# Short second halves of two experts: three products in two 64-column tiles instead of rounded part and rest side by side

## The chip, the cores and the metric

The kernel runs on one core of a Trainium2 chip. The metric is the device time of one execution in microseconds, lower is better. TensorE multiplies a stationary operand (its weights, loaded by a LDWEIGHTS) with a moving one and writes to PSUM; VectorE and ScalarE work between PSUM and SBUF; GpSimd (POOL in the rows) issues the indirect DMAs; SyncE (SP) issues the others.

## What is computed

Two stages, cut to what matters here. First a decaying linear attention over 2 batches, 8 heads, 768 positions and 64 dimensions; its output is 1536 tokens of 512 values. Then a mixture of 8 experts: each token goes to one expert `e` (its own best one or the one of the token before it), and

```python
h = np.maximum(x[b, s] @ w1[e], 0.0)     # 512 -> 1024
out[b, s] = p[e] * (h @ w2[e])           # 1024 -> 512, p the softmax of the logits
```

All inputs and outputs are f32.

## The kernel before

The matmuls of the experts run in f16. Each f32 operand is split into a rounded part (`hi`, `hh`) and the rest that rounding left (`lo`, `hl`), and a product of two operands is the sum of three f16 products: rounded by rounded, rounded by rest, rest by rounded.

The tokens are sorted into lists of up to 256 places an expert, gathered by an indirect DMA and turned by a DMA transpose. The first two experts are taken as they come, the other six are ranked by the number of their tokens; `CAPS` gives the places that each position in this order computes: 256 for the first three, then 244, 228, 214, and 192 for the last two, positions 6 and 7. A list is worked on in two halves, places 0 to 127 and the others. At positions 6 and 7 the second half has 192 - 128 = 64 places; `stacked(e)` is true for these two alone.

For each position, in the order of the program:

- `up(e, f)`, for 8 blocks `f` of 128 hidden values: twelve matmuls (L764) into one PSUM tile of 128 hidden values by the list's places. ScalarE writes `hh`, the positive part in f16, and VectorE writes the rest `hl`. Where `stacked(e)`, ScalarE's instruction stands at L774, and VectorE's is two (L777): the rest of places 0 to 127 goes to `hl`, and that of places 128 to 191 into the 64 free columns of `hh` right behind the rounded part of the same places. So 128 columns of `hh` hold rounded part and rest of the short second half side by side.
- `down(e, hf, f)`, for the half `hf` and the same 8 blocks: an ordinary half has three matmuls a block (L823), with 128 (or fewer) columns of `hh` or `hl` as weights and 512 columns of `w2` moving. The short second half of a stacked position has two (L814, L815): the 128 columns side by side, against the rounded `w2` and against its rest. Partitions 0 to 63 of the PSUM tile then hold the sum from the rounded part, and 64 to 127 that from the rest.
- `store(e, hf)`: scales by the probability and scatters the rows by an indirect DMA. For the short half ScalarE first copies partitions 64 to 127 (L844), VectorE adds the two halves (L845) and scales (L846).

At positions 6 and 7 the short second half comes ahead of the first half. At position 7, the last, the first half is computed in two parts of 256 columns, so that storing the first part overlaps the second. The order of everything is the order of the program text: a schedule by hand (`ORDER`) up to the first experts, and the loops at the end of the program from there. Weights are loaded by SyncE, rounded by ScalarE (L161) and their rest is taken by VectorE (L169), a few pieces behind each block.

In the attention part, earlier in the program, f32 matmuls use less than the whole array: L469 (scores by values) and L516 (the state) have 64 columns of weights each and write in turn to partitions 0 to 63 and 64 to 127 of one PSUM bank. L428 is a full-width f32 matmul (a transpose) of 128 moving columns.

Of the kernel before, what the change touches and what calls it, by code (L numbers as in the profile page):

```python
# [11 lines left out]
AF = mybir.ActivationFunctionType  # L12
ALU = mybir.AluOpType
# [4 lines left out]
P = 128  # L18
HP = P // 2
# [9 lines left out]
KF = F // P  # L29
# [77 lines left out]
def moe_kernel(ctx: ExitStack, tc, q, k, v, w_gate, w_local, w1, w2, cst, out):  # L107
    nc = tc.nc
# [73 lines left out]
    def ready(u, i):  # L182
        while any(tuple(t[:2]) == (u, i) for t in todo):
            split_some(1)
# [127 lines left out]
    with ExitStack() as both:  # L312
# [74 lines left out]
        def bank(b):  # L387
            pool, tag = BANKS[b]
            return pool.tile([P, NP, P], F32, tag=tag, name="tr")
# [273 lines left out]
        def rows(e, hf):  # L663
            return CAPS[e] - P if hf else P
# [56 lines left out]
        XX, HH, PO, RELU = {}, {}, {}, ([], [])  # L721
# [3 lines left out]
        def half(what, e, hf):  # L725

            t_ = what[e, hf] if (e, hf) in what else what[e]
            return t_ if (e, hf) in what else t_[..., hf * P : (hf + 1) * P]
# [14 lines left out]
        def up(e, f, hf=None, part=None):  # L743

            pair_, n_ = (f % 2, P) if hf is not None else (0, CAPS[e])
            first, last = part != 1, part != 0
            if f == 0 and first:
                if e < FEW and hf == 0:
                    HH[e, 0] = [
                        ap_.tile([P, KF, P], F16, tag="eh", name=f"{n}{e}_0", bufs=4) for n in ("hh", "hl")  # L750
                    ]
                else:
                    HH[e] = [mp[0].tile([P, KF, CAP], F16, tag=n, name=f"{n}{e}", bufs=2) for n in ("hh", "hl")]
            if first and pair_ == 0:
                third = hf is None and f % 3 == 2
                HH["ps"] = (ps_1 if third else ps_sc).tile([P, 2 * P], F32, tag="lgb" if third else "sc", name="h")
            ready(2 * e, 7)
            xx = XX[e] if hf is None else half(XX, e, hf)
            wh, wl = units[2 * e]
            ps, fs = HH["ps"], slice(f * P, (f + 1) * P)  # L760
            terms = [(kk, a, b_) for kk in range(KD) for a, b_ in ((wh, 0), (wh, 1), (wl, 0))]
            for n in range(0 if first else 6, 12 if last else 6):
                kk, a, b_ = terms[n]
                nc.tensor.matmul(  # L764
                    ps[:, pair_ * P : pair_ * P + n_], lhsT=a[:, kk, fs], rhs=xx[:, b_, kk, :n_],
                    start=(n == 0 and pair_ == 0), stop=(n == 11), skip_group_check=True,
                )
            if not last or (hf is not None and pair_ == 0):
                return
            if hf is None:  # L770
                hh, hl = (h_[:, f, :n_] for h_ in HH[e])
                ps = ps[:, :n_]
                if stacked(e):
                    nc.scalar.activation(hh, ps, AF.Relu)  # L774
                    both_ = ((hl[:, :P], slice(0, P)), (HH[e][0][:, f, P + HP :], slice(P, n_)))
                    for to, cols in both_:
                        nc.vector.scalar_tensor_tensor(to, ps[:, cols], 0.0, hh[:, cols], ALU.max, ALU.subtract)  # L777
                    return
            else:
                ps = ps.rearrange("p (a b) -> p a b", a=2)  # L780
                hh, hl = (h_[:, f - 1 : f + 1, :] for h_ in halves(e, hf))
            relu = [
                lambda: nc.scalar.activation(hh, ps, AF.Relu),  # L783
                lambda: nc.vector.scalar_tensor_tensor(hl, ps, 0.0, hh, ALU.max, ALU.subtract),  # L784
            ]
            if e < FEW and hf == 0:
                for to, op in zip(RELU, relu):
                    to.append(op)
                return
            for op in relu:  # L790
                op()

        def halves(e, hf):
            return HH[e, hf] if (e, hf) in HH else [h_[..., hf * P : (hf + 1) * P] for h_ in HH[e]]

        def stacked(e):

            return e >= FEW and CAPS[e] - P == HP

        def down(e, hf, f, part=None):  # L800
            ready(2 * e + 1, f)
            wh, wl = units[2 * e + 1]
            hh, hl = halves(e, hf)
            if f == 0:
                if part is not None:
                    to = bank("ys"[part]).rearrange("p a b -> p (a b)")[:, : DM // 2]
                    PO[e, hf] = PO.get((e, hf), []) + [to]
                elif hf == 0 and mp:
                    PO[e, hf] = ps_1.tile([P, DM], F32, tag="y", name="o")
                else:  # L810
                    PO[e, hf] = ps_tr.tile([P, DM], F32, tag="tr", name="o")
            if hf and stacked(e):
                po, a = PO[e, hf], HH[e][0][:, f, P:]
                nc.tensor.matmul(po, lhsT=a, rhs=wh[:, f, :], start=(f == 0), stop=(f == KF - 1), skip_group_check=True)  # L814
                nc.tensor.matmul(po, lhsT=a, rhs=wl[:, f, :], start=False, stop=(f == KF - 1), skip_group_check=True)  # L815
                return
            m = rows(e, hf)
            po = (PO[e, hf] if part is None else PO[e, hf][part])[:m]
            cols = slice(0, DM)
            if part is not None:  # L820
                cols = slice(part * DM // 2, (part + 1) * DM // 2)
            for n, (a, b_) in enumerate(((hh, wh), (hh, wl), (hl, wh))):
                nc.tensor.matmul(  # L823
                    po, lhsT=a[:, f, :m], rhs=b_[:, f, cols], start=(f == 0 and n == 0), stop=(f == KF - 1 and n == 2)
                )
# [37 lines left out]
        for e in range(FEW):  # L863
            fillers += [lambda e=e, f=f, h=h: up(e, f, 0, h) for f in range(KF) for h in range(2)]
            fillers += [lambda e=e, f=f: down(e, 0, f) for f in range(KF)]
# [45 lines left out]
        for e in range(FEW):  # L911
            if e + 1 < FEW:
                transposed(e + 1, 1)
            transposed(e + 2, 0)
            transposed(e + 2, 1)
            for f in range(KF):
                up(e, f, 1)
                split_some(1, 2 * e + 3)
                if e == 0 and f == 3:
                    fill_table(ptab, T["prhs"], 0, NC, 2 * E)  # L920
                    LST["pt"] = ranked(cp, probs(cp, ptab, 2.0 ** -(SH + SW + SP), ""), "ptr")
                    for n in range(FEW):
                        store(n, 0)
            queue(2 * e + 5)
            for f in range(KF):
                down(e, 1, f)
                split_some(1, 2 * e + 4)
            store(e, 1)
            queue(2 * e + 6)
        for e in range(FEW, LAST):  # L930
            if e + 2 < E:
                transposed(e + 2, 0)
                transposed(e + 2, 1)
            for f in range(KF):
                up(e, f)
                split_some(1, 2 * e + 3)
            queue(2 * e + 5)
            for n, hf in enumerate((1, 0) if stacked(e) else (0, 1)):
                if e + 1 == E and n == 1:
                    for part in range(2):  # L940
                        for f in range(KF):
                            down(e, hf, f, part)
                    store(e, hf)
                    break
                for f in range(KF):
                    down(e, hf, f)
                    if f % 2 == 1:
                        split_some(1, 2 * e + 4)
                store(e, hf)
            queue(2 * e + 6)  # L950
# [5 lines left out]
    with tc.If(nmore > 0), tc.For_i(0, nmore, 1), ExitStack() as lo_:  # L956
# [12 lines left out]
        for e in range(E):  # L969
# [18 lines left out]
            for f in range(KF):  # L988
                ps = pa.tile([P, CAP], F32, tag="h2p", name="h2p")
                for kk in range(KD):  # L990
                    nc.tensor.matmul(
                        ps, lhsT=wa[:, kk, f * P : (f + 1) * P], rhs=x2[:, kk, :],
                        start=(kk == 0), stop=(kk == KD - 1),
                    )
                nc.scalar.activation(h2[:, f, :], ps, AF.Relu)
            for hf in range(2):
                po = pa.tile([P, DM], F32, tag="tr2", name="o2")
                for f in range(KF):
                    nc.tensor.matmul(
                        po, lhsT=h2[:, f, hf * P : (hf + 1) * P], rhs=wb[:, f, :],  # L1000
                        start=(f == 0), stop=(f == KF - 1),
# [33 lines left out]
```

## Time and profile before

| | us |
|---|---|
| time, median of 3 runs | 268.12 (262.58 to 271.2) |
| the profiled execution's own time | 261.32 |
| its span, first to last instruction | 259.5 |
| TensorE matmul busy | 234.5 (90%) |
| weight loads busy | 176.3 (68%) |
| VectorE busy | 161.0 (62%) |
| ScalarE busy | 131.1 (51%) |
| GpSimd busy | 64.3 (25%) |

The rows come from one execution, and start at its first instruction. A matmul's own length in a row is longer than the step from one start to the next, since matmuls are pipelined and their ends are modelled; what a stream of them costs is read from starts. Weight loads (PEld) run beside matmuls. In a row of a timeline, neighbours of one line are merged: the start of the first, the time from it to the last end, and their count behind an x. A form such as 128*64 128x512 is the rows by columns of the weights, then the partitions and columns that move.

### The profile page before, as it was taken

The numbers are of one execution on the slowest core, as the hardware profiler recorded it, in microseconds if no ns is written. First come the engines' busy times: TensorE is split into PE (matmuls) and PEld (weight loads), VectorE is DVE, ScalarE is ACT, GpSimd is POOL, SyncE is SP. The second block draws the span as 40 slices with busy tenths as digits, with TensorE's granted clock in tenths as the row PEclk, the third lists the DMA queues.
The fourth block names the chain that finished last, engine by engine and source line by source line (L and its number), as shares of the span: only waits on it lengthen the run. The fifth ranks groups of instructions, "written<-read, shape, count | busy, mean of one in ns | idle before, by whom it ended". The sixth has DMA issues, their size and how long they took to land. (4 is left out here: it accounts for less than half of the span.)

```text
span 259.5 us, 6195 instructions
## 1 busy us (share of the span) xinstructions
PE 234.5 (90%) x2420; PEld 176.3 (68%) x2420; DVE 161.0 (62%) x383; ACT 131.1 (51%) x262; POOL 64.3 (25%) x69
## 2 busy tenths in 40 slices
PE   8588888867998989899999999999999999999970
PEld 2477667756887865858667847947947947849650
DVE  1247669877789878205997963965864865922210
ACT  2139877556442121213896763765765765803210
POOL 2440541624360104314025212042101103011020
PEclk9779999996899999999999999999999999999996
DMA  6999999999899744999999999999999994101001
GB/s 166 199 324 360 335 289 276 267 346 226 212 211 199 193 135 154 338 119 174 362 379 269 381 260 254 397 292 340 404 160 399 270 301 151 25 12 40 4 12 45
DMA packets 74004, 60.20 MB, mean 232 GB/s; under 512 B 51820, under 2 KB 58220, under 8 KB 73968
## 3 DMA queue, kind: packets, MB, share of 16 engines
q1 hardware_dynamic: 70992, 52.39, 74.9%
q0 software_dynamic: 2976, 7.35, 9.4%
q8 instruction: 21, 0.34, 0.6%
q14 instruction: 15, 0.12, 0.1%
HBM read 47.66 MB, written 6.91 MB: 210 GB/s over the span
## 5 line engine op out<-in xcount | busy, mean ns | idle before, releaser
L169 DVE SCALAR_TENSOR_TENSOR lo<-stg,hi 128x512 f16<-128x512 f32 x128 | 85.4, 701 | 16.0 <-ACT hi L161 13.2
L161 ACT ACTIVATE hi<-stg 128x512 f16<-128x512 f32 x128 | 73.7, 621 | 9.9 <-DMA stg<-in_moe_w_dram 9.9
L764 PE MATMUL h<-xx,hi 128*128 128x128 f16 (+5 forms) x640 | 77.8, 242 | 0.0
L764 PE MATMUL h<-xx,lo 128*128 128x128 f16 (+5 forms) x320 | 71.7, 242 | 0.0
L764 PEld LDWEIGHTS <-hi 128*128 128x128 f16 x640 | 55.9, 98 | 3.8 <-issue 0.3
L853 POOL DMA_INDIRECT out_dram<-ob,sidx x16 | 18.4, 1148 | 93.4 <-ACT ob L852 26.4
L823 PE MATMUL o<-hi,hl 128*128 128x512 f16 (+3 forms) x104 | 39.4, 379 | 1.1 <-DVE hl L784 1.1
L823 PEld LDWEIGHTS <-hh 128*128 128x128 f16 (+3 forms) x240 | 24.6, 103 | 21.9
L823 PE MATMUL o<-hi,hh 128*128 128x512 f16 (+3 forms) x104 | 39.4, 379 | 0.0
L823 PE MATMUL o<-lo,hh 128*128 128x512 f16 (+3 forms) x104 | 39.4, 379 | 0.0
L784 DVE SCALAR_TENSOR_TENSOR hl<-h,hh 128x256 f16<-128x256 f32 (+3 forms) x48 | 19.5, 407 | 22.9 <-ACT hh L783 22.5
L764 PEld LDWEIGHTS <-lo 128*128 128x128 f16 x320 | 31.3, 98 | 0.6
L783 ACT ACTIVATE hh<-h 128x256 f16<-128x256 f32 (+3 forms) x48 | 17.8, 372 | 22.0 <-PE h L764 21.8
L669 POOL DMA_INDIRECT xg<-xs,gidx x16 | 16.2, 1014 | 30.4 <-DMA xx<-xg 23.9
L823 PEld LDWEIGHTS <-hl 128*128 128x128 f16 (+3 forms) x120 | 12.4, 103 | 13.3 <-DVE hl L784 1.6
L370 POOL TENSOR_TENSOR ks<-ink,ct 128x512 f32<-128x512 f32 (+1 forms) x13 | 15.1, 1171 | 24.9 <-DMA ink<-in_k_dram 20.9
L448 DVE TENSOR_TENSOR am<-sc,ct 128x512 f32<-128x512 f32 x24 | 15.4, 685 | 8.7 <-PE sc L443 8.6
L852 ACT ACTIVATE ob<-o,ptr 128x512 f32<-128x512 f32 (+3 forms) x11 | 7.5, 685 | 22.9 <-issue 16.6
L443 PE MATMUL sc<-qT,kT 64*128 64x128 f32 x192 | 15.7, 309 | 2.9 <-ACT kT L379 2.9
L443 PEld LDWEIGHTS sc<-qT,kT 64*128 64x128 f32 x192 | 13.3, 210 | 4.9 <-ACT kT L379 3.9
L361 POOL TENSOR_TENSOR qs<-inq,ct 128x1024 f32<-128x1024 f32 (+1 forms) x7 | 11.8, 1685 | 17.3 <-DMA inq<-in_q_dram 15.5
L379 ACT ACTIVATE kT<-tr 128x512 f32<-128x512 f32 (+1 forms) x12 | 6.7, 561 | 15.1 <-PE tr L428 15.0
(135 smaller groups left out, 239.1 us busy)
## 6 DMA issues: line engine op xcount, KB each, us to landing
stg<-in_moe_w_dram SPq DMA_DIRECT2D x64, 512.0 KB, 7.8
inv<-in_v_dram SPq DMA_DIRECT2D x12, 256.0 KB, 6.3
xs<-xr SPq DMA_DIRECT2D x12, 256.0 KB, 5.3
ink<-in_k_dram SPq DMA_DIRECT2D x11, 256.0 KB, 5.9
inq<-in_q_dram SPq DMA_DIRECT2D x5, 512.0 KB, 6.1
inq<-in_q_dram SPq DMA_DIRECT2D x2, 256.0 KB, 5.1
ct<-in_constants_dram SPq DMA_DIRECT2D x1, 260.0 KB, 3.2
ink<-in_k_dram SPq DMA_DIRECT2D x2, 128.0 KB, 2.6
```

The source lines that it names most:

```text
L161: nc.scalar.activation(hi, stg, AF.Copy, scale=2.0**SW)
L169: nc.vector.scalar_tensor_tensor(lo, stg, 2.0**SW, hi, ALU.mult, ALU.subtract)
L361: eng.tensor_tensor(T["qs", c][:, :, hs].rearrange("t two h d -> t h two d"), src.rearrange("t h (two d) -> t h two d", two=2), tb[:, hs]. ...
L370: eng.tensor_tensor(T["ks", c][:, hs], src, tb.unsqueeze(2).to_broadcast([P, n, D]), ALU.mult)
L443: nc.tensor.matmul(scs[j][:, p, :], lhsT=kT[r, p, :], rhs=qT[r, p, :], start=True, stop=True)
L448: nc.vector.tensor_tensor(T["am", c][j], T["sc", c][j], mask_.unsqueeze(1).to_broadcast([P, NP, P]), ALU.mult)
L669: nc.gpsimd.indirect_dma_start(out=xg, out_offset=None, in_=xs[:top, :], in_offset=bass.IndirectOffsetOnAxis(ap=ix[:, hf * E + e : hf * E ...
L764: nc.tensor.matmul(ps[:, pair_ * P : pair_ * P + n_], lhsT=a[:, kk, fs], rhs=xx[:, b_, kk, :n_], start=(n == 0 and pair_ == 0), stop=(n == ...
L783: lambda: nc.scalar.activation(hh, ps, AF.Relu),
L784: lambda: nc.vector.scalar_tensor_tensor(hl, ps, 0.0, hh, ALU.max, ALU.subtract),
L823: nc.tensor.matmul(po, lhsT=a[:, f, :m], rhs=b_[:, f, cols], start=(f == 0 and n == 0), stop=(f == KF - 1 and n == 2))
L853: nc.gpsimd.indirect_dma_start(out=out[:, :], out_offset=bass.IndirectOffsetOnAxis(ap=LST["sidx"][:m, at_ : at_ + 1], axis=0), in_=ob[:m], ...
```

## The change

In `up`, the special case for stacked positions goes: ScalarE writes `hh` and VectorE writes `hl` for all 192 places, one instruction each. In `down`, the short second half is computed from the three usual products, with 64 columns of weights a matmul. Nothing is done at an even block; at an odd one the six matmuls of two blocks are issued, and they write in turn to partitions 0 to 63 and 64 to 127. `store` stays: it adds the two halves of the tile, which now each hold half of the products. The product of rest by rest, which the side-by-side form brought along, is no longer computed.

```diff
                 hh, hl = (h_[:, f, :n_] for h_ in HH[e])
                 ps = ps[:, :n_]
-                if stacked(e):
-                    nc.scalar.activation(hh, ps, AF.Relu)
-                    both_ = ((hl[:, :P], slice(0, P)), (HH[e][0][:, f, P + HP :], slice(P, n_)))
-                    for to, cols in both_:
-                        nc.vector.scalar_tensor_tensor(to, ps[:, cols], 0.0, hh[:, cols], ALU.max, ALU.subtract)
-                    return
...
             if hf and stacked(e):
-                po, a = PO[e, hf], HH[e][0][:, f, P:]
-                nc.tensor.matmul(po, lhsT=a, rhs=wh[:, f, :], start=(f == 0), stop=(f == KF - 1), skip_group_check=True)
-                nc.tensor.matmul(po, lhsT=a, rhs=wl[:, f, :], start=False, stop=(f == KF - 1), skip_group_check=True)
+                po = PO[e, hf]
+                if f % 2:
+                    last = f == KF - 1
+                    terms = [(hh, wh, f - 1), (hh, wl, f - 1), (hl, wh, f - 1), (hh, wl, f), (hh, wh, f), (hl, wh, f)]
+                    for n, (a, b_, i) in enumerate(terms):
+                        nc.tensor.matmul(
+                            po[n % 2 * HP : n % 2 * HP + HP], lhsT=a[:, i, :HP], rhs=b_[:, i, :],
+                            start=(f == 1 and n < 2), stop=(last and n > 3), skip_group_check=True,
+                        )
                 return
```

TensorE, the start of position 6's short second half (`hi` and `lo` are the two parts of its `w2`, `hh` and `hl` those of its hidden values; the form is the output's). Before, two blocks of 128 hidden values:

```order
L814 LDWEIGHTS hh_3193
L814 MATMUL o<-hi_2984,hh_3193 128x512
L815 LDWEIGHTS hh_3193
L815 MATMUL o<-lo_2985,hh_3193 128x512
L814 LDWEIGHTS hh_3193
L814 MATMUL o<-hi_2984,hh_3193 128x512
L815 LDWEIGHTS hh_3193
L815 MATMUL o<-lo_2985,hh_3193 128x512
```

The same two blocks after the change:

```order
L812 LDWEIGHTS hh_3193
L812 MATMUL o<-hi_2984,hh_3193 64x512
L812 LDWEIGHTS hh_3193
L812 MATMUL o<-lo_2985,hh_3193 64x512
L812 LDWEIGHTS hl_3194
L812 MATMUL o<-hi_2984,hl_3194 64x512
L812 LDWEIGHTS hh_3193
L812 MATMUL o<-lo_2985,hh_3193 64x512
L812 LDWEIGHTS hh_3193
L812 MATMUL o<-hi_2984,hh_3193 64x512
L812 LDWEIGHTS hl_3194
L812 MATMUL o<-hi_2984,hl_3194 64x512
```

Four matmuls that write 128 partitions became six that write 64 each, and `hl` is now read here too. Over the stage it is 16 before and 24 after, at both positions, in the same place between `up` and the first half.

VectorE, the first three blocks of position 6's `up` (L169 takes the rest of a weight piece). Before:

```order
L777 SCALAR_TENSOR_TENSOR hl_3194<-h,hh_3193 128x128
L777 SCALAR_TENSOR_TENSOR hh_3193<-h,hh_3193 128x64
L169 SCALAR_TENSOR_TENSOR lo_3212<-stg_0_3107,hi_3211 128x512
L777 SCALAR_TENSOR_TENSOR hl_3194<-h,hh_3193 128x128
L777 SCALAR_TENSOR_TENSOR hh_3193<-h,hh_3193 128x64
L169 SCALAR_TENSOR_TENSOR lo_3212<-stg_0_3107,hi_3211 128x512
L777 SCALAR_TENSOR_TENSOR hl_3194<-h,hh_3193 128x128
L777 SCALAR_TENSOR_TENSOR hh_3193<-h,hh_3193 128x64
L169 SCALAR_TENSOR_TENSOR lo_3212<-stg_1_3109,hi_3211 128x512
```

After:

```order
L778 SCALAR_TENSOR_TENSOR hl_3194<-h,hh_3193 128x192
L169 SCALAR_TENSOR_TENSOR lo_3211<-stg_0_3107,hi_3210 128x512
L778 SCALAR_TENSOR_TENSOR hl_3194<-h,hh_3193 128x192
L169 SCALAR_TENSOR_TENSOR lo_3211<-stg_0_3107,hi_3210 128x512
L778 SCALAR_TENSOR_TENSOR hl_3194<-h,hh_3193 128x192
L169 SCALAR_TENSOR_TENSOR lo_3211<-stg_1_3109,hi_3210 128x512
```

Two instructions a block became one, 16 in all over the two positions. ScalarE, GpSimd and SyncE issue the same instructions in the same order as before.

## Rows read from the trace of the kernel before

**Rows 1.** The page's 40 slices of the span, busy tenths and granted clock:

```profile
PE   8588888867998989899999999999999999999970
...
PEclk9779999996899999999999999999999999999996
DMA  6999999999899744999999999999999994101001
```

**Rows 2.** Busy time by stretch: stretch, length, engines (count), clock, DMA share, GB/s:

```profile
core 0: us, PE busy (x) PEld busy (x) DVE busy (x) ACT busy (x) POOL busy (x), PEclk, DMA share, GB/s
195.00:251.10 56.10, 56.10 (x458) 41.98 (x456) 29.01 (x72) 26.39 (x58) 6.99 (x7) 1.00 0.46 138
225.69:229.15 3.46, 3.46 (x20) 1.57 (x18) 1.77 (x5) 0.91 (x3) 0.00 (x0) 1.00 0.04 15
242.25:245.70 3.45, 3.45 (x18) 1.57 (x17) 0.42 (x2) 0.33 (x1) 0.00 (x0) 1.00 0.03 7
```

**Rows 3.** Timeline of TensorE, ends of the two stages, and last matmul:

```profile
225.69 0.38 PE L814 MATMUL o<-hi,hh 128*128 128x512 f16 x1
...
229.15 0.38 PE L823 MATMUL o<-hi,hh 128*128 128x512 f16 x1
...
242.25 0.38 PE L814 MATMUL o<-hi,hh 128*128 128x512 f16 x1
...
245.70 0.27 PE L823 MATMUL tr<-hi,hh 128*128 128x256 f16 x1
...
250.83 0.27 PE L823 MATMUL tr<-hi,hl 128*128 128x256 f16 x1
```

**Rows 4.** Timeline of ScalarE and GpSimd, their last rows:

```profile
251.14 0.48 ACT L852 ACTIVATE ob<-tr,ptr 128x256 f32<-128x256 f32 x1 [2.14 <-PE tr L823]
251.89 0.99 POOL L853 DMA_INDIRECT out_dram<-ob,sidx  x1 [2.98 <-ACT ob L852]
```

**Rows 5.** Timeline of TensorE, short windows around two changes of form:

```profile
73.94 0.49 PE L428 MATMUL tr<-ct,ks 128*128 128x128 f32 x3
74.36 0.33 PE L469 MATMUL y<-am,inv 128*64 128x128 f32 x2
...
75.51 0.40 PE L516 MATMUL st<-inv,ks 128*64 128x64 f32 x8
75.84 0.33 PE L428 MATMUL tr<-ct,ks 128*128 128x128 f32 x1
```

**Rows 6.** Timeline of TensorE, one chunk's L469 as a whole:

```profile
74.36 1.09 PE L469 MATMUL y<-am,inv 128*64 128x128 f32 x16
```

**Rows 7.** Line L469: ns min/median/max, first and last start, forms:

```profile
L469 PEld LDWEIGHTS y<-am,inv x192: 132/137/138, 18.0 to 89.7; 128*64 128x64 f32 x192
L469 PE MATMUL y<-am,inv x192: 272/273/323, 18.0 to 89.8; 128*64 128x128 f32 x192
```

**Rows 8.** Groups by line and form: count, busy us, mean ns, idle before:

```profile
L814 PE MATMUL o<-hi,hh 128*128 128x512 f16 x16 | 6.1, 379 | 0.0
L777 DVE SCALAR_TENSOR_TENSOR hl<-h,hh 128x128 f16<-128x128 f32 x16 | 4.6, 288 | 11.4 <-ACT hh L774 11.4
L777 DVE SCALAR_TENSOR_TENSOR hh<-h,hh 128x64 f16<-128x64 f32 x16 | 3.4, 214 | 0.0
L784 DVE SCALAR_TENSOR_TENSOR hl<-h,hh 128x214 f16<-128x214 f32 x8 | 3.0, 374 | 2.9 <-ACT hh L783 2.9
L823 PEld LDWEIGHTS <-hh 128*100 128x100 f16 x16 | 2.0, 125 | 1.5
L823 PEld LDWEIGHTS <-hh 128*86 128x86 f16 x16 | 1.9, 119 | 1.6
L814 PEld LDWEIGHTS <-hh 128*128 128x128 f16 x16 | 1.6, 98 | 1.7
```

**Rows 9.** Timeline of VectorE and ScalarE, the last hidden block of each position:

```profile
226.39 0.28 DVE L777 SCALAR_TENSOR_TENSOR hl<-h,hh 128x128 f16<-128x128 f32 x1
...
242.45 0.33 ACT L774 ACTIVATE hh<-h 128x192 f16<-128x192 f32 x1 [0.66 <-PE h L764]
242.81 0.29 DVE L777 SCALAR_TENSOR_TENSOR hl<-h,hh 128x128 f16<-128x128 f32 x1 [0.57 <-ACT hh L774]
```

## The prediction

> **What bounds the kernel now.** I read first how the engines are loaded over the span, to find which one the end of the program waits for. In the last sixth the DMA engines are nearly idle, while TensorE stays busy up to the last two slices and its granted clock full up to the last one [rows 1]. Then the stages: from 195 us to the end of its last matmul TensorE has no idle time, at a granted clock of 1.00 [rows 2]. The two stages that the change rewrites are the short second halves of the experts at positions 6 and 7. They run from 225.69 to 229.15 us and from 242.25 to 245.70 us, 16 matmuls each, L814 and L815 in turn (16 of each in all [rows 8]), one every 0.216 us (3.46 / 16) [rows 2, 3]; the counts in rows 2 also hold neighbours that reach into a stretch. Both lie on the path: the matmuls that follow have all their operands and start at once, the last one starts at 250.83 us, ScalarE takes its result at 251.14 us, and GpSimd issues the last store at 251.89 us after 2.98 us of waiting for ScalarE [rows 3, 4]. What TensorE gains or loses in the two stages therefore moves the end by the same amount. The profiled execution took 261.32 us, of which 259.5 us are its span.
>
> **What the change removes.** 2 x 16 matmuls of 512 moving columns with 128-column weights: 3.46 + 3.45 = 6.91 us [rows 2]. Their fourth product, rest of the activation by rest of the weights, goes with them.
>
> **What it adds on TensorE.** 2 x 24 matmuls of 512 moving columns with 64-column weights, written in turn to partitions 0 to 63 and 64 to 127 of one bank. The price hangs on whether two neighbours run side by side. No row shows that in f16, but the attention part does it in fp32, with weights of 128x64 and outputs in the two halves of one bank. There two matmuls of at most 0.323 us each fill together a row of 0.33 us [rows 5, 7], so they start at most 0.01 us apart. The 16 of one chunk take 1.09 us [rows 6]: less 0.27 for the last one's own length and 0.05 for the first one's extra length (323 against 273 ns [rows 7]), 7 pair steps of 0.11 us remain. Full-width fp32 matmuls of the same 128 columns also step by 0.11 us each ((0.49 - 0.27) / 2 [rows 5]). A pair costs what one costs. In f16 a pair then costs 0.216 us, and 24 pairs 5.18 us. The upper bound of this reading is 0.01 us more on each pair for the second start: 0.24 us in all. I take 5.18, since the 7 steps of rows 6 already contain such starts. The nearest row differs in type, so I looked at what could not carry over. In fp32 a column takes 0.11 us / 128 = 0.85 ns and brings 4 bytes a partition, in f16 0.216 us / 512 = 0.42 ns and 2 bytes: the two streams together need about 9.5 bytes a ns from each partition in both cases. PSUM takes 128 partitions of f32 every 0.42 ns, as it does for a full matmul now.
>
> **What the change of tiling costs.** Going into the 64-column form and coming out of it does not pipeline like a normal step. In attention the last full-width matmul starts at 73.94 + 0.49 - 0.27 = 74.16 us and the first 64-column one at 74.36 us: 0.20 where the step was 0.11 us. On the way out the last one starts at 75.51 + 0.40 - 0.22 = 75.69 and the full-width one at 75.84 us, 0.07 us ahead of the former's modelled end, just as on the way in [rows 5]. The next matmul thus starts when the last is 0.07 us from its end. A 512-column matmul is modelled at 0.379 us [rows 8], so the next starts 0.379 - 0.07 = 0.31 us after it in place of 0.216: 0.09 us for a switch, 0.37 us for the four. The first matmul after a switch also waits for its own weights: 0.05 us in fp32 [rows 7]. For f16 the bounds are nothing and a whole load. A load is 98 ns at 128 columns, 125 at 100 and 119 at 86 columns, which drawn on gives an estimate of 110 ns at 64 [rows 8]. I take the fp32 row's 0.05, 0.20 us for four; the bounds are 0 and 0.44 us. Between the switches a load of 110 ns lies under a pair of 216 ns, as the loads of 119 ns lie today under single matmuls of 216 ns.
>
> **What moves elsewhere.** On VectorE two instructions a block of 128 hidden columns (288 and 214 ns) become one of 192 columns. From 288 ns at 128 and 374 at 214 columns that is an estimate of 352 ns [rows 8], 0.15 us less, sixteen times. It is worth nothing, because TensorE waits for none of them. What they must now meet is the last pair. At position 7 the last rest is then done at 242.81 + 0.35 = 243.16 us [rows 9] by the old times, and the first use of it is in the twelfth pair, 242.25 + 0.09 + 11 x 0.216 = 244.72 us: 1.5 us to spare. At position 6 it is 226.39 + 0.35 = 226.74 against 225.69 + 2.47 = 228.16 us. The eighth block's rounded part (ScalarE, 242.45 + 0.33 us) is first used in the eleventh pair and has 1.7 us. If that cover were gone, the wait would be what is missing from these slacks. SP and GpSimd issue the same rows in the same order, and no queue is passed. The sum of the two halves and their store are unchanged and come earlier with TensorE.
>
> **The sum.** 6.91 - 5.18 - 0.37 - 0.20 = 1.16 us less: 261.32 becomes 260.2 us, or 0.4%. With the bounds the gain is 1.73 us at most (switches free) and 6.91 - 5.18 - 0.24 - 0.37 - 0.44 = 0.68 us at least.
>
> **Rivals.**
> - *The weight loads show.* If each pair, not only the first after a switch, waits 0.05 us for its loads, 24 pairs cost 1.20 us more, and with the switches 1.73 - 1.20 - 0.37 = 0.16 us remain: 261.2 us. The change decides for itself up to a pair of (6.91 - 0.57) / 24 = 0.264 us. For it speaks that loads narrower than 128 columns are longer already now, 119 and 125 against 98 ns [rows 8]; against it that the fp32 pairs hide two loads of 137 ns [rows 7] under a step of 0.11 us. The Trainium skill, TensorEngine Tiling, "Restrictions and Gotchas", says that column tiling excludes Fast Weight Load, a rule against this change. The loads of 86 and 100 columns here are not tiled and long as well, so by the trace the width alone already brings it about; by the rule the 64-column loads stay near 110 ns, which is the estimate used above. The Trainium skill, TensorE: Matmul & The Clock Gate, "Measured speedup vs the span model", gives 2.38 for three column tiles, 0.79 of full use; as an estimate two such tiles would give 1.59, a pair of 0.272 us, and 261.5 us with the switches. The fp32 rows here show no such loss.
> - *The tiles take turns.* If two f16 streams can't be fed at once, 48 matmuls at 0.216 us take 10.37 us, 3.46 us more than now, with 0.57 for the switches 4.0 us: 265.4 us, 1.5% slower. It becomes a loss from the same 0.264 us a pair. Only the type of the operands speaks for it; the bytes above speak against it.
> - *The end doesn't follow.* If something other than TensorE set the last store, the time stays 261.3 us. ScalarE's start 0.04 us after the last matmul's modelled end (250.83 + 0.27) and GpSimd's wait for ScalarE speak against it [rows 3, 4].
>
> **How the numbers follow.** Forecast 0.80, loads that show 0.09, tiles in turn 0.07, end not moved 0.04. All four lie between -0.7% and +1.5% of 261.32 us, inside the 2% that a measurement of this kernel can tell from no change. What decides the absolute time is the spread of the runs: the three shown are 262.58, 268.12 and 271.2, the profiled one 261.32 us, so the median shown is 2.6% above the execution that I sum against. For a median of a few such runs I take the middle of the four, (262.58 + 268.12) / 2 = 265.35 us, less 1.16: 264.2 us. The range goes from the lowest run with the largest gain, 261.32 - 1.73 = 259.6, to the highest with the smallest, 271.2 - 0.68 = 270.5 us; the turn-taking rival on the middle run, 269.4 us, lies in it. Beyond 2% could fall: slower 0.05, mostly the turn-taking tiles in a run pair that differs by chance; faster 0.03 by chance alone; the same 0.92.
>
> **What would show it.** In the profile after: rows of x2 with two starts some 0.01 us apart in both stages and pair steps of 0.216 us; the first full-width matmul behind each stage 0.31 to 0.36 us after the start of the last 64-column one; no idle time on TensorE behind VectorE's L778; and from the first matmul of position 6's short half to ScalarE's last row about 24.2 us in place of 25.45 (251.14 - 225.69), since the first switch's 0.09 us lies ahead of that matmul. Steps of 0.216 us for every single matmul would prove the turn-taking right, pairs of about 0.27 us the loads.

## The result and the profile after

| | before | changed |
|---|---|---|
| time, median, us | 262.58 (262.03 to 271.2, 5 runs) | 260.24 (259.02 to 266.61, 5 runs) |
| ratio to the kernel before, with its 95% interval | | 0.990 (0.986 to 0.994) |
| the profiled execution's own time / span, us | 261.32 / 259.5 | 264.51 / 262.7 |

In this comparison the changed kernel is about 1% faster; a ratio of 1 lies outside the interval, and so does a gain of 2%. How much of that is the change's own is taken up at the end of the experiments. The medians are of all executions, but each ratio, here and below, compares only those within 1.5% of the fastest of their kernel, which the profiled one of the changed kernel is not. In that execution position 6's up-projection starts at 222.39 us in place of 217.77. So the two traces are compared from that matmul on, with lengths and not with times from the start of the span. The first row is the start of that stretch in the kernel before; its last matmul stands in rows 3.

```profile
217.77 0.33 PE L764 MATMUL h<-xx,hi 128*128 128x192 f16 x2
```

The same stretch of the changed kernel in the timeline of TensorE: its first matmul, the first and the last of position 6's short half with the full-width one behind it, the same of position 7, and the last matmul of all.

```profile
222.39 0.33 PE L764 MATMUL h<-xx,hi 128*128 128x192 f16 x2
...
230.22 0.25 PE L764 MATMUL h<-xx,lo 128*128 128x192 f16 x1
230.40 0.40 PE L812 MATMUL o<-hi,hh 128*64 128x512 f16 x1
230.40 0.40 PE L812 MATMUL o<-lo,hh 128*64 128x512 f16 x1
230.64 0.38 PE L812 MATMUL o<-hi,hl 128*64 128x512 f16 x1
230.64 0.38 PE L812 MATMUL o<-lo,hh 128*64 128x512 f16 x1
230.86 0.38 PE L812 MATMUL o<-hi,hh 128*64 128x512 f16 x1
230.86 0.38 PE L812 MATMUL o<-hi,hl 128*64 128x512 f16 x1
...
232.80 0.38 PE L812 MATMUL o<-hi,hh 128*64 128x512 f16 x1
232.80 0.38 PE L812 MATMUL o<-hi,hl 128*64 128x512 f16 x1
233.11 0.39 PE L823 MATMUL o<-hi,hh 128*128 128x512 f16 x1
233.34 0.38 PE L823 MATMUL o<-lo,hh 128*128 128x512 f16 x1
...
246.32 0.40 PE L812 MATMUL o<-hi,hh 128*64 128x512 f16 x1
...
248.72 0.38 PE L812 MATMUL o<-hi,hl 128*64 128x512 f16 x1
249.03 0.28 PE L823 MATMUL tr<-hi,hh 128*128 128x256 f16 x1
...
254.17 0.27 PE L823 MATMUL tr<-hi,hl 128*128 128x256 f16 x1
```

Nearly every time stands twice: two matmuls of 64 columns start together, within 0.01 us, then the next two 0.216 us later ((232.80 - 230.64) / 10, from the second of the twelve pairs to the last). From the first matmul of position 6's up-projection to the last of all it is 254.17 - 222.39 = 31.78 us, against 250.83 - 217.77 = 33.06 before [rows 3]: 1.28 us less. The way in takes 0.18 us from the last full-width matmul (230.22 to 230.40) where these stepped by 0.08, and the way out 0.31 us (232.80 to 233.11).

Line L812 (ns min/median/max, first and last start, forms; the last two rows say what ended the idle time before it, us and how often), and the groups by line and form that answer to rows 8 (count, busy us, mean ns, idle before):

```profile
L812 PEld LDWEIGHTS <-hh x32: 106/110/110, 230.4 to 248.5; 128*64 128x64 f16 x32
L812 PE MATMUL o<-hi,hh x16: 379/379/403, 230.4 to 248.7; 128*64 128x512 f16 x16
L812 PE MATMUL o<-lo,hh x16: 379/379/403, 230.4 to 248.5; 128*64 128x512 f16 x16
...
  ACT hi L161: 0.2, 1
  issue: 0.2, 1
```

```profile
L778 DVE SCALAR_TENSOR_TENSOR hl<-h,hh 128x192 f16<-128x192 f32 x16 | 5.7, 354 | 12.0 <-ACT hh L777 12.0
L812 PE MATMUL o<-hi,hl 128*64 128x512 f16 x16 | 4.8, 379 | 0.0
```

A load of 64 columns takes 110 ns, VectorE's 192 columns 354 ns, and no matmul of the new stages that reads `hl` waits for it (idle 0.0). The two short idle times of the weight loads are the two ways in. One is put down to ScalarE's `hi` of L161; but the weights loaded there are `hh`, and in the kernel before the same instruction was done only after the stage's first matmul had started (225.13 + 0.62 = 225.75 us, against 225.69 in rows 3):

```profile
225.13 0.62 ACT L161 ACTIVATE hi<-stg 128x512 f16<-128x512 f32 x1
```

Position 7's wait, of the same 0.2 us, has no such name (`issue`). A short wait that appears at every change of form is the change's, whatever releaser stands beside it.

The end (timelines of ScalarE and GpSimd, which answer to rows 4) follows as before: ScalarE starts 0.31 us after the last matmul, GpSimd 0.75 us after ScalarE:

```profile
254.48 0.47 ACT L852 ACTIVATE ob<-tr,ptr 128x256 f32<-128x256 f32 x1 [2.15 <-PE tr L823]
255.23 0.99 POOL L853 DMA_INDIRECT out_dram<-ob,sidx  x1 [3.08 <-ACT ob L852]
```

### The profile page after: what moved, and what is told of

Read it like the earlier page. It is cut to its first block, busy times and chain, and to the rows that moved or that the text cites. A ratio compares the mean times of both kernels' runs of the same rounds, so it can differ in the third digit from the quotient of the medians.

```text
span 262.7 us, 6205 instructions
## 1 busy us (share of the span) xinstructions
PE 234.7 (89%) x2436; PEld 177.0 (67%) x2436; DVE 163.6 (62%) x367; ACT 130.1 (49%) x262; POOL 63.8 (24%) x69
## 3 DMA queue, kind: packets, MB, share of 16 engines
HBM read 47.66 MB, written 6.91 MB: 208 GB/s over the span
## 5 line engine op out<-in xcount | busy, mean ns | idle before, releaser
L169 DVE SCALAR_TENSOR_TENSOR lo<-stg,hi 128x512 f16<-128x512 f32 x128 | 86.7, 712 | 15.4 <-ACT hi L161 11.9
L161 ACT ACTIVATE hi<-stg 128x512 f16<-128x512 f32 x128 | 73.0, 620 | 3.3 <-DMA stg<-in_moe_w_dram 3.3
L778 DVE SCALAR_TENSOR_TENSOR hl<-h,hh 128x256 f16<-128x256 f32 (+4 forms) x64 | 25.2, 394 | 35.2 <-ACT hh L777 34.4
L777 ACT ACTIVATE hh<-h 128x256 f16<-128x256 f32 (+4 forms) x64 | 23.2, 362 | 29.8 <-PE h L764 28.5
L669 POOL DMA_INDIRECT xg<-xs,gidx x16 | 17.6, 1103 | 31.0 <-DMA xx<-xg 19.7
L443 PE MATMUL sc<-qT,kT 64*128 64x128 f32 x192 | 16.7, 323 | 2.2 <-ACT kT L379 2.1
L370 POOL TENSOR_TENSOR ks<-ink,ct 128x512 f32<-128x512 f32 (+1 forms) x13 | 13.4, 1032 | 19.6 <-DMA ink<-in_k_dram 12.7
L443 PEld LDWEIGHTS sc<-qT,kT 64*128 64x128 f32 x192 | 14.1, 222 | 4.3 <-ACT kT L379 3.3
L469 PE MATMUL y<-am,inv 128*64 128x128 f32 x192 | 14.6, 301 | 0.6 <-DVE am L448 0.6
```

What stands on the lines that cost most here:

```text
L161: nc.scalar.activation(hi, stg, AF.Copy, scale=2.0**SW)
L169: nc.vector.scalar_tensor_tensor(lo, stg, 2.0**SW, hi, ALU.mult, ALU.subtract)
L370: eng.tensor_tensor(T["ks", c][:, hs], src, tb.unsqueeze(2).to_broadcast([P, n, D]), ALU.mult)
L443: nc.tensor.matmul(scs[j][:, p, :], lhsT=kT[r, p, :], rhs=qT[r, p, :], start=True, stop=True)
L469: nc.tensor.matmul(y, lhsT=T["v", c][:, hd, :], rhs=am[j][:, p, :], start=(c % NCH == 0 and p == 0), stop=(p == NP - 1), skip_group_check= ...
L669: nc.gpsimd.indirect_dma_start(out=xg, out_offset=None, in_=xs[:top, :], in_offset=bass.IndirectOffsetOnAxis(ap=ix[:, hf * E + e : hf * E ...
```

## The experiments

Two things had to be told apart: whether the pairing of tiles is what pays, and whether the measured 1% (2.3 us between the medians) is more than the 1.28 us of the trace. Below, "the stretch" is from the first matmul of position 6's up-projection to the last matmul of all, in the profiled execution; each ratio is of measured times, to the kernel before measured beside it; six, mixed and two_dve have one execution each and no ratio.

| kernel | start of the stretch, us | its length, us | ratio, 95% interval |
|---|---|---|---|
| before | 217.77 | 33.06 | |
| null | 220.70 | 33.05 | 1.0047 (0.997 to 1.012) |
| changed | 222.39 | 31.78 | 0.990 (0.986 to 0.994) |
| again | 220.89 | 31.78 | 0.9952 (0.989 to 1.002) |
| again2 | 222.78 | 31.79 | 0.9913 (0.987 to 0.995) |
| one_tile | 215.75 | 36.96 | 1.0202 (1.013 to 1.027) |
| grouped | 219.69 | 31.80 | 0.9962 (0.988 to 1.005) |
| six | 216.02 | 32.70 | |
| far | 220.78 | 35.29 | 1.0028 (0.998 to 1.008) |
| mixed | 221.79 | 32.47 | |
| merged | 220.88 | 31.55 | 0.9947 (0.990 to 0.999) |
| two_dve | 226.29 | 31.78 | |

**All in one tile.**

```diff
-                            po[n % 2 * HP : n % 2 * HP + HP], lhsT=a[:, i, :HP], rhs=b_[:, i, :],
+                            po[:HP], lhsT=a[:, i, :HP], rhs=b_[:, i, :],
...
```

with `start` and `stop` moved to the first and the last of the 24, and the store taking one half of the tile alone, without the copy and the sum.

> The same 24 matmuls a position with 64 columns of weights, but all of them into partitions 0 to 63, so that no two can run side by side; the store takes the one half and leaves out the copy and the sum of two halves. Theory A (a pair of tiles is what pays): every matmul steps by 0.216 us, each stage takes 24 x 0.216 = 5.18 us and the time is 48 x 0.216 - 6.91 + 0.45 = 3.9 us above the kernel before, 1.5%. Rival (64 columns of weights are cheaper by themselves, or the loads are the price): steps clearly under or over 0.216 us, and the two stages differ from 5.2 us.

Timeline of TensorE, the start of position 6's short half:

```profile
223.76 0.40 PE L812 MATMUL o<-hi,hh 128*64 128x512 f16 x1
224.00 0.38 PE L812 MATMUL o<-lo,hh 128*64 128x512 f16 x1
224.22 0.38 PE L812 MATMUL o<-hi,hl 128*64 128x512 f16 x1
```

One start at a time, 0.22 us apart. The stretch is 36.96 us: 3.90 more than before, as expected, and 5.18 more than in the changed kernel, which is 24 steps of 0.216. The same matmuls without a second tile are a loss of 1.5% by the trace and 2% by the measured time, so the pairing is the whole gain.

**Three in a row for each tile.**

```diff
-                            po[n % 2 * HP : n % 2 * HP + HP], lhsT=a[:, i, :HP], rhs=b_[:, i, :],
+                            po[n // 3 * HP : n // 3 * HP + HP], lhsT=a[:, i, :HP], rhs=b_[:, i, :],
...
```

with `start` and `stop` moved to the first and the last matmul of each tile.

> The same products in the same two tiles, but three matmuls in a row for one tile and then three for the other, in place of turn by turn. Theory A (matmuls start in their order, so only neighbours in different tiles overlap): of six matmuls only those at the two borders pair, six take four steps of 0.216 us, each stage takes 16 steps plus one, about 3.6 us, and the time is that of the kernel before plus the switches, +0.4 to +0.7 us. Rival (each tile runs its own queue): three steps for six matmuls, a stage of 2.6 to 3.0 us and the changed kernel's time, 1.3 us under the kernel before.

My theory failed here. The stretch is 31.80 us, that of the changed kernel, and the timeline of TensorE shows pairs from the first:

```profile
227.71 0.40 PE L812 MATMUL o<-hi,hh 128*64 128x512 f16 x1
227.72 0.61 PE L812 MATMUL o<-lo,hh 128*64 128x512 f16 x2
227.96 0.38 PE L812 MATMUL o<-hi,hh 128*64 128x512 f16 x1
```

The row at 227.72 us holds two `lo,hh`, the first of which starts there, so two different matmuls started at 227.71 and 227.72. The program has `hi,hh`, `lo,hh`, `hi,hl` for the first tile and then `lo,hh` for the second. In one tile matmuls start 0.22 us apart (one_tile), so the `lo,hh` at 227.72 is the second tile's: it went ahead of two that wait for theirs. How far that reaches became the next question.

**Twelve in a row, and six.**

```diff
-                if f % 2:
...
+                t = f // 4 * HP
+                for n, (a, b_) in enumerate(((hh, wh), (hh, wl), (hl, wh))):
+                    nc.tensor.matmul(
+                        po[t : t + HP], lhsT=a[:, f, :HP], rhs=b_[:, f, :],
...
```

(`f // 2 % 2` in place of `f // 4` for six; `start` and `stop` are again at the first and the last matmul of each tile).

> The same products in the same two tiles, with twelve matmuls in a row for the first tile (hidden blocks 0 to 3) and then twelve for the second. The run with three in a row paired as well as turn by turn, so matmuls do not have to be neighbours. Theory A (TensorE takes matmuls of a free tile ahead of waiting ones, within a queue that holds at least 24 matmuls and loads): a stage of 2.6 to 3.0 us, the changed kernel's time. Rival (it looks only a few instructions ahead): the first tile's matmuls run alone for most of the stage, 4 to 5.2 us a stage, and the time is 1 to 4 us above the kernel before.

> The same products in the same two tiles, six matmuls in a row for one tile and then six for the other. With three in a row all paired; with twelve in a row the thirteenth matmul, the first of the second tile, started with the ninth and the stage took twenty steps. Theory A (a matmul for the free tile is taken if it stands at most four places behind the oldest waiting one): two matmuls alone, four pairs, two, then four pairs, two alone, 14 steps of 0.216 us and 2.8 us from the first to the last start of a stage, against 2.40 us for the changed kernel. Rival (the reach is one of the kernel's data, such as the wait for the fifth hidden block, and not of places): 12 steps and 2.4 us, or 16 and more.

Timeline of TensorE with twelve in a row:

```profile
228.79 0.40 PE L810 MATMUL o<-hi,hh 128*64 128x512 f16 x1
229.04 0.38 PE L810 MATMUL o<-lo,hh 128*64 128x512 f16 x1
...
230.33 0.38 PE L810 MATMUL o<-lo,hh 128*64 128x512 f16 x1
230.55 0.38 PE L810 MATMUL o<-hi,hl 128*64 128x512 f16 x1
230.55 0.59 PE L810 MATMUL o<-hi,hh 128*64 128x512 f16 x2
230.79 0.56 PE L810 MATMUL o<-lo,hh 128*64 128x512 f16 x2
231.01 0.56 PE L810 MATMUL o<-hi,hl 128*64 128x512 f16 x2
231.22 0.38 PE L810 MATMUL o<-hi,hh 128*64 128x512 f16 x1
...
232.95 0.38 PE L810 MATMUL o<-hi,hl 128*64 128x512 f16 x1
```

Eight matmuls run alone. The ninth starts at 230.55 us, and with it the thirteenth, the first of the second tile; then the tenth to twelfth have partners, and the last eight are alone again. 20 steps, 4.16 us from the first to the last start against 2.40 in the changed kernel. The rival held: the reach is short. The thirteenth started with the ninth, from which it stands four places away in the program, and not with the eighth, five places away. On that rule the run with six in a row was forecast at 14 steps and 2.8 us. Its timeline of TensorE, the ends of the first stage:

```profile
224.03 0.40 PE L810 MATMUL o<-hi,hh 128*64 128x512 f16 x1
224.27 0.38 PE L810 MATMUL o<-lo,hh 128*64 128x512 f16 x1
224.49 0.38 PE L810 MATMUL o<-hi,hl 128*64 128x512 f16 x1
224.49 0.59 PE L810 MATMUL o<-hi,hh 128*64 128x512 f16 x2
...
226.89 0.38 PE L810 MATMUL o<-hi,hl 128*64 128x512 f16 x1
```

Two run alone, the third starts with the seventh, and the stage has 14 steps and takes 2.86 us from the first to the last start; the stretch is 0.92 us longer than the changed kernel's (four steps of 0.216 are 0.86). What counts the four places, matmuls or the eight instructions with their loads, was not tried.

**More changes of form, and fewer.** Position 6 with its halves block by block, and position 6's short half moved ahead of position 7's:

```diff
+            if e + 2 == E:
+                for f in range(KF):
+                    for hf in (1, 0):
+                        down(e, hf, f)
...
```

> Position 6's two halves block by block: six 64-column matmuls after every two blocks of the first half, so that position 6 has eight switches in place of two. Theory A (a switch costs 0.12 us going in and 0.11 us going out wherever it stands): six switches more, +0.68 us, 32.45 us from the start of position 6's up-projection to the last matmul in place of 31.78. Rival (the price is that of a stage's start, such as the first wait for a hidden block, and not of the form): 31.8 us.

```diff
+            if e + 1 == E:
+                for f in range(KF):
+                    down(e - 1, 1, f)
+                store(e - 1, 1)
...
```

(position 7's short half is given another bank here).

> The changed kernel with position 6's short second half moved behind position 7's up-projection, right ahead of position 7's own, so that there is one stay in the 64-column form in place of two. Theory A (each entry costs 0.12 and each way out 0.11 us, and nothing else does): 0.23 us less from the start of position 6's up-projection to the last matmul, 31.55 in place of 31.78 us, and a ratio to the kernel before of 0.994, which the spread can't tell from 0.995. Rival (the switches cost nothing or the moved half opens a wait): 31.78 us, or more with a gap ahead of the moved matmuls.

Timeline of TensorE in the first of the two, one way in and one out:

```profile
230.14 0.38 PE L823 MATMUL o<-hi,hl 128*128 128x512 f16 x1
230.45 0.40 PE L812 MATMUL o<-hi,hh 128*64 128x512 f16 x1
...
230.69 0.38 PE L812 MATMUL o<-hi,hl 128*64 128x512 f16 x1
...
230.91 0.38 PE L812 MATMUL o<-hi,hl 128*64 128x512 f16 x1
231.22 0.39 PE L823 MATMUL o<-hi,hh 128*128 128x512 f16 x1
231.45 0.38 PE L823 MATMUL o<-lo,hh 128*128 128x512 f16 x1
```

0.31 us each way in place of a step of 0.216, and 0.02 more on the first step behind the way in (0.24, from 230.45 to 230.69), 0.01 behind the way out (0.23, from 231.22 to 231.45). Six switches more made the stretch 32.47 us (32.45 expected), two fewer 31.55 (31.55 expected): 0.115 us a switch both times (0.69 / 6 and 0.23 / 2). The second kernel is the best of all by its trace, 1.51 us shorter in the stretch than the kernel before; by its measured ratio (0.9947) it can't be told from the changed one.

**VectorE's part undone.**

```diff
+            if hf is None and stacked(e):
+                relu[1:] = [
+                    lambda c=c: nc.vector.scalar_tensor_tensor(hl[:, c], ps[:, c], 0.0, hh[:, c], ALU.max, ALU.subtract)
+                    for c in (slice(0, P), slice(P, P + HP))
+                ]
```

> The changed kernel with VectorE's rest taken by two instructions a block again (places 0 to 127 and 128 to 191). Theory A (VectorE's saving is worth nothing): 31.78 us from the start of position 6's up-projection to the last matmul, and no idle time on TensorE behind VectorE. Rival (the shorter VectorE work carries part of the gain): up to 1 us more, with TensorE waiting for the rest hl.

31.78 us, to the hundredth that of the changed kernel: VectorE's saving is worth nothing. (The execution as a whole took 268.41 us; its stretch starts at 226.29.)

**The size in measured time.** The kernel before with only a comment added (null), and the changed kernel twice with only a comment added.

> The kernel before against itself (one comment added), to see what the measurement makes of no change. Theory A: a ratio between 0.995 and 1.005, with an interval that may miss 1 by some tenths of a per cent, since the fast runs of one kernel already spread by 1 us. Theory B: a ratio within 0.998 to 1.002, so that a ratio of 0.99 can't be chance.

> The changed kernel once more, to separate two readings of the measured gain of about 1% (2.6 us), which is more than the 1.28 us by which the profile's last stages became shorter. Theory A (the gain is TensorE's alone: 24 pairs in place of 32 matmuls, less four switches): 1.28 us, a ratio of 0.995, and the surplus of the first measurement was chance in the attention part; from the start of position 6's up-projection to the last matmul 31.8 us as in the first profile. Theory B (something ahead of these stages got faster too): a ratio of 0.99 again, and the start of position 6's up-projection more than 1 us earlier than in the kernel before at the same granted clock.

> The changed kernel a third time, for the size of the gain on the clock: two measurements gave 0.990 and 0.9952, and the kernel before against itself 1.0047. Theory A (1.28 us from TensorE's last stages): 0.995, and 31.78 us from the start of position 6's up-projection to the last matmul. Theory B (about 2.6 us): 0.99.

No change at all measured 1.0047. The three measurements of the changed kernel are 0.990, 0.9952 and 0.9913; 1.28 us of 262.5 are 0.9951. For more than these 1.28 us stands that two of three intervals end below or at 0.995. Against it stands that the start of the stretch is no earlier: 222.39, 220.89 and 222.78 us in the three profiles of the changed kernel, 217.77 and 220.70 in the two of the kernel before, and that other kernels missed their trace's difference by as much in either direction: one_tile measured 1.0202 where its stretch says 1.015, far 1.0028 where it says 1.0085. Theory B's earlier start was not found.

The record also has the mean granted clock of TensorE for each execution, and it bears on this. Busy time by stretch, columns as in rows 2, for the profiles with the earliest and the latest start, one_tile and two_dve; in each the first row is the part ahead of the stretch:

```profile
0.00:215.75 215.75, 199.18 (x2125) 148.07 (x2125) 149.31 (x339) 117.33 (x232) 55.92 (x64) 0.98 1.02 275
215.75:252.90 37.15, 37.15 (x313) 27.79 (x311) 12.11 (x26) 11.28 (x27) 4.28 (x4) 1.00 0.06 16
...
0.00:226.29 226.29, 206.87 (x2124) 154.66 (x2125) 151.53 (x339) 117.26 (x232) 56.55 (x64) 0.94 0.95 262
226.29:258.30 32.01, 32.01 (x313) 25.22 (x311) 13.76 (x44) 12.46 (x29) 4.28 (x4) 1.00 0.07 19
```

In all twelve profiles the clock within the stretch is 1.00, the upper of its two levels (2.4 GHz); ahead of it the mean is 0.98 in one_tile and 0.94 in two_dve. In rows 1 the slices with the low clock are among or right behind those in which TensorE is least busy (0.5, and 0.6 and 0.7). Of the ratios of the changed kernel, again compares executions of equal mean clock (0.971 on both sides) and gives 0.9952; again2 compares 0.971 with 0.969. The misses of null (0.968 against 0.971), one_tile (0.969 against 0.971) and far (0.975 against 0.969) have the sign of their clocks as well; those of grouped (0.974 against 0.971) and merged (0.972 against 0.969) have not. As an estimate, a straight line through time and clock of the 76 executions of the kernel before and the changed one whose clock is on record (comments aside) puts 0.01 of mean clock at 2.6 us, and the changed kernel 1.6 us (0.9 to 2.2, 95%) under the kernel before at the same clock. That fits the 1.28 us of the trace and not the 2.6 of theory B. No run here sets the clock, so the surplus of single comparisons is put down to it by this estimate and not by an experiment.

## Why the prediction was right, and where its sizes were off

- **The bound.** Right: what TensorE gained in the two stages came out at the end, and ScalarE's last row came 24.08 us (254.48 - 230.40) after the first matmul of position 6's short half, 24.2 forecast.
- **The pair's price.** Right, and the fp32 rows of the attention part were the right place to read it: pairs in f16 step by 0.216 us. The upper bound of 0.01 us a pair was not needed. Neither the loads (pairs of 0.264 us and more) nor turn-taking showed; one_tile shows what the latter would have cost, 3.90 us against the 4.0 worked out.
- **The switch.** The 0.09 us by which the next matmul starts later was right each time. The term that was too big is the one for the first matmul's own load: 0.05 us taken over from fp32 for each of four switches. It is 0.403 - 0.379 = 0.024 us going in, and by the longer first full-width matmul (0.39 for 0.38) about 0.01 going out: 0.07 us in all in place of 0.20. With it the sum is 6.91 - 5.18 - 0.37 - 0.07 = 1.29 us, and the trace shows 1.28; the forecast was 1.16. That the load is what makes the first matmul longer was a reading in the prediction, and no run here separates it from the rest of the switch.
- **The loads.** They are 110 ns at 64 columns against 98 at 128, as the prediction had it from the 86 and 100 columns of rows 8. Under a pair of 216 ns that is hidden. The Trainium skill, TensorEngine Tiling, "Restrictions and Gotchas", excludes Fast Weight Load under column tiling; no run here shows what that costs beyond these lengths. The Trainium skill, TensorE: Matmul & The Clock Gate, "Measured speedup vs the span model", has 2.38 for three column tiles, from which the prediction estimated a pair of 0.272 us; the pairs here take 0.216 us, so no loss of that kind appears.
- **VectorE.** Right: 354 ns for the estimated 352, and two_dve shows that none of it counts.
- **The time.** 260.24 us is inside 259.6 to 270.5, but 4 us under the 264.2 forecast; 2.8 us of that is the anchor's, the time that the forecast starts from, and 1.2 us the gain's. The step that failed is the middle of four executions, 265.35 us, taken as the typical run of the kernel before; its median in this comparison was 262.58. Four values with a spread of 10 us do not fix a middle. That the time lies in the range says little for the mechanism: the range is 11 us wide and holds the turn-taking rival's 269.4 us as well. It is the pairs and the length of the stretch that bear the forecast out. The ratio by the sum was 1 - 1.16 / 261.32 = 0.9956, just outside the measured interval of 0.986 to 0.994; the chance of 0.92 for a change within 2% was the right part of it.

## What to carry to other kernels

Where half of the weight columns are empty, two column tiles run two products in the time of one, and a stay in the 64-column form costs about 0.23 us, in and out. A pair of 512 moving columns saves a step of 0.216 us over the same two matmuls in one tile, so by these numbers it pays from the second pair on, if the stage is on the path. Read the price of a pair from any other stage that already writes to the two halves of a bank, even in another type, and collect such stages into one stay where the order allows it. For a change of half a per cent compare lengths within the stage that changed, and executions of the same granted clock; the measured time of the kernel before differed from itself by about as much (1.0047).

## What was not expected of the hardware

- The two tiles need not take turns in the program. A matmul for the free tile started ahead of up to three waiting ones of the other tile: with three in a row all 24 paired, with six in a row 20 of 24, with twelve in a row 8 of 24 (12, 14 and 20 steps). The Trainium skill, TensorE: Matmul & The Clock Gate, "The mechanism", has matmuls start and end strictly in their order; these traces differ, and they decide.
- At a change of form the next matmul starts 0.07 us before the modelled end of the last, after f16 matmuls of 192 and of 512 columns and after the fp32 ones of rows 5. What differs is how much longer the first one is: 0.024 us going in and 0.01 going out in f16, up to 0.05 in fp32 [rows 7].
- The executions of one program text differ by 10 us, and the profiles put that ahead of position 6, where the granted clock varies: the start of the stretch lies anywhere from 215.75 to 226.29 us in the twelve profiles, while the stretch of one program repeats to 0.01 us.
